# All sums on VectorE, attention steps spread over fixed units, and one output tile of block 0 split between two stages

## Chip, cores, metric

One core of a Trainium2 chip. The metric is device time in microseconds (us); several runs are taken, and all times compared here are of runs in the fast state (within 1.5% of the fastest run of the same kernel). The kernel before takes 316.09 us (median of 4 runs, 315.37 to 317.78).

## Reference

```python
kv  = einsum('bhsd,bhse->bhde', k, v)           # 8 batches, 8 heads, 576 positions, head size 64
o   = einsum('bhsd,bhde->bhse', q, kv)
x   = o / sqrt(mean(o*o, -1) + 1e-6) * g_norm   # as [4608 tokens, 512]
h   = x @ w_in                                  # [4608, 2048]
out = (max(h,0) + alpha*min(h,0)) @ w_out       # [4608, 512]
```

## The kernel before, where it matters

Tokens are handled in nine blocks of 512. In block w, sixteen *units* each make one hidden group of 128 rows (four matmuls, line 335; ScalarE and VectorE evict it into `gt`), seven output matmuls of block w-1 (line 486), and a share of the attention of block w+1. For a pair of heads the attention steps are `t` (transposes of q, line 236), `kv` (product of k and v, line 254), `ot` (q times kv, line 277) and `ssq` (sums of squares, line 293), after which VectorE writes `xt`, the input of the next block's hidden groups. To evict is to read a finished PSUM bank, so that it can be filled again. The output product is done with seven half-size products in place of eight, for which sums of activations (`s1` to `s4`) and of w_out (`wsum`) are needed. (In block 1, and in the stage before it, block 0's output is still made in the plain way, by line 360.) Two engines make the sums; GpSimd also issues nearly all loads and, from batch 2 on, regroups each loaded batch.

```python
# stage_p has bufs=2: a staging tile is free again when batch b-2 has been read from it
def load_main(b, nm, h0, h1): nc.gpsimd.dma_start(out=st, in_=...)             # q, k, v of a batch
def regroup(b, nm, h0, h1, eng): eng.tensor_copy(out=bufs[b % 3][nm]..., in_=stages[b, nm]...)
# v is not regrouped: step_kv reads vst, the staging tile, directly
...
def s_sum(w, n, k):
    if n == 1:   nc.vector.tensor_add(out=t, in0=a21, in1=a22)
    elif n == 2: nc.vector.tensor_sub(out=t, in0=sums[w,1,k], in1=a11)
    elif n == 3: nc.gpsimd.tensor_sub(out=t, in0=a11, in1=a21)
    else:        (nc.gpsimd if w == 1 else nc.vector).tensor_sub(out=t, in0=a12, in1=sums[w,2,k])
...
# PSUM bank Z takes product 5, is read ("c22") in unit 12, then takes product 3 (from unit 13 on)
Y_READS = {2: ("p1",), 5: ("u2",), 7: ("c11",), 9: ("u3",), 12: ("c22",), 14: ("c21",)}
...
for w in range(1, NW):
    if w + 2 < B: load_batch(w + 2)              # GpSimd's queue: k, v, q
    for u in range(NF):
        m1_group(w, G_ORDER[u])
        unit_sums(w, u)
        if w + 2 < B and u in (10, 12): regroup(w + 2, "k" if u == 10 else "q", 0, H, nc.gpsimd)
        ...                                      # seven prod_mm, then Y_READS
        while steps and n - len(steps) < want: steps.pop(0)()     # attention steps, as they fit
```

## Time and profile before

| | busy us of 314.3 | in the changed kernel, of 318.3 |
|---|---|---|
| TensorE (PE) | 287.0 | 290.4 |
| VectorE (DVE) | 219.3 | 231.7 |
| ScalarE (ACT) | 161.1 | 160.2 |
| GpSimd (POOL) | 127.2 | 62.9 |

How to read it: TensorE bounds the kernel, so what counts is what makes it wait, stage by stage. Below I measure a block from the start of its first line-335 matmul to the next block's, in TensorE's timeline. The lines of the profile that show the waits are in the prediction.

### The profile page before, as it was taken

What the parts mean: (1) busy time and instruction counts of PE and PEld (TensorE: products, weight loads), DVE (VectorE), ACT (ScalarE), POOL (GpSimd) and SP (SyncE); (2) the same over time, 40 slices, a digit from 0 to 9 for tenths busy, and PEclk for the clock granted to TensorE, in tenths of its full rate; (3) what the DMA queues carried; (4) which work ended last, traced back from release to release, by engine and by line L of the source; (5) the groups of instructions that cost most, each with busy time, mean ns of one, the idle gap of its engine ahead of it and who ended that gap; (6) DMA issues with size and microseconds to landing.
All of it is one profiled execution on the core that took longest, in us unless ns stands there. A gap on an engine that the chain in (4) does not pass through costs nothing.

```text
span 314.3 us, 5166 instructions
## 1 busy us (share of the span) xinstructions
PE 287.0 (91%) x1972; PEld 180.7 (57%) x1972; DVE 219.3 (70%) x373; ACT 161.1 (51%) x268; POOL 127.2 (40%) x118
## 2 busy tenths in 40 slices
PE   5778899696899999999999999999999999999992
PEld 1433354343466657665766576656665666666682
DVE  4358833758769886888688768876777778866831
ACT  2256556466455556555655555555654565444210
POOL 8424312999999551365136413311111112211100
PEclk9999999979799999999999999999999999999998
DMA  7999999790049199029902990111102110200233
GB/s 109 181 206 194 200 199 214 110 155 2 28 43 185 39 149 177 1 41 161 161 17 27 157 162 9 26 67 34 37 1 52 50 35 9 75 19 33 64 89 85
DMA packets 52552, 28.32 MB, mean 90 GB/s; under 512 B 15136, under 2 KB 52016, under 8 KB 52528
## 3 DMA queue, kind: packets, MB, share of 16 engines
q0 software_dynamic: 40320, 18.16, 45.8%
q1 hardware_dynamic: 11424, 9.19, 10.3%
q10 hardware_dynamic: 784, 0.66, 0.8%
q8 instruction: 15, 0.25, 0.3%
q14 instruction: 9, 0.07, 0.1%
HBM read 36.71 MB, written 9.44 MB: 147 GB/s over the span
## 4 chain that ended last, share of the span: by engine, by line
PE 76%; DVE 12%; ACT 5%; issue 2%; DMA 2%; SPq 1%; DVEq 0%
PE h_ps L335 34%; PE yY L486 11%; PE yZ L486 9%; PE yX L486 7%; DVE gt L346 4%; PE qt_ps L236 3%; DVE s L433 3%; ACT m_sb L342 3%; PE ot_ps L277 3%; PE ssq_ps L293 2%; PE kv_ps L254 2%; DMA alpha_row<-in_moe_alpha_dram 2%; DVE s L435 1%; ACT sq_sb L283 1%; DVE y_sb L513 1%
## 5 line engine op out<-in xcount | busy, mean ns | idle before, releaser
L335 PE MATMUL h_ps<-xt,w_in_sb 128*128 128x512 f16 x576 | 148.9, 384 | 2.2 <-DVE gt L346 1.4
L346 DVE SCALAR_TENSOR_TENSOR gt<-m_sb,beta_sb,h_ps 128x512 f16<-128x512 f32 x144 | 107.0, 744 | 56.7 <-ACT m_sb L342 55.3
L342 ACT ACTIVATE m_sb<-h_ps 128x512 f32<-128x512 f32 x144 | 85.9, 597 | 81.3 <-PE h_ps L335 73.5
L437 POOL TENSOR_TENSOR s<-gt 128x512 f16<-128x512 f16 x32 | 39.1, 1223 | 134.5 <-DVE gt L346 134.2
L335 PEld LDWEIGHTS <-w_in_sb 128*128 128x128 f16 x576 | 54.8, 99 | 55.3 <-issue 12.1
L486 PEld LDWEIGHTS <-s 128*128 128x128 f16 x512 | 50.1, 98 | 21.1 <-issue 1.9
L486 PEld LDWEIGHTS <-gt 128*128 128x128 f16 x384 | 37.6, 98 | 15.1 <-issue 0.4
L303 DVE SCALAR_TENSOR_TENSOR xt<-ot_ps,g2col,rstd 128x512 f16<-128x512 f32 x36 | 26.9, 746 | 12.2 <-ACT rstd L295 12.1
L486 PE MATMUL yX<-w_out_sb,gt 128*128 128x256 f16 x256 | 35.1, 273 | 0.1
L295 ACT ACTIVATE rstd<-ssq_ps,eps_t 128x512 f32<-128x512 f32 x36 | 24.7, 687 | 16.5 <-PE ssq_ps L293 16.3
L283 ACT ACTIVATE sq_sb<-ot_ps 128x512 f16<-128x512 f32 x36 | 21.4, 598 | 16.4 <-PE ot_ps L277 16.4
L248 ACT COPY qt_sb<-qt_ps 128x576 f16<-128x576 f16 x28 | 17.9, 638 | 15.3 <-PE qt_ps L236 15.3
L440 DVE TENSOR_TENSOR s<-gt,s 128x512 f16<-128x512 f16 x28 | 21.2, 758 | 0.0
L236 PE MATMUL qt_ps<-ident,qsb 128*128 128x128 f16 x160 | 14.5, 226 | 6.0 <-DVE kv_sb L262 5.2
L293 PE MATMUL ssq_ps<-sq_sb,mask 128*128 128x512 f16 x36 | 13.7, 382 | 5.8 <-ACT sq_sb L283 4.5
L433 DVE TENSOR_TENSOR s<-gt 128x512 f16<-128x512 f16 x32 | 18.8, 588 | 0.0
L486 PE MATMUL yY<-w_out_sb,s 128*128 128x256 f16 x128 | 18.7, 272 | 0.1
L486 PE MATMUL yZ<-w_out_sb,s 128*128 128x256 f16 x128 | 17.5, 272 | 0.7 <-DVE y_sb L513 0.3
L486 PE MATMUL yY<-wsum,s 128*128 128x256 f16 x128 | 17.6, 273 | 0.0
L486 PE MATMUL yZ<-wsum,s 128*128 128x256 f16 x128 | 17.6, 273 | 0.0
L486 PE MATMUL yY<-wsum,gt 128*128 128x256 f16 x128 | 17.6, 273 | 0.0
L236 PEld LDWEIGHTS <-qsb 128*128 128x128 f16 x160 | 11.8, 101 | 9.8 <-issue 5.9
(66 smaller groups left out, 263.9 us busy)
## 6 DMA issues: line engine op xcount, KB each, us to landing
out_dram<-y_sb SPq DMA_DIRECT2D x72, 64.0 KB, 2.2
kst<-in_k_dram POOLq DMA_DIRECT2D x7, 512.0 KB, 6.4
qst<-in_q_dram POOLq DMA_DIRECT2D x7, 512.0 KB, 11.8
vst<-in_v_dram POOLq DMA_DIRECT2D x7, 512.0 KB, 9.2
out_dram<-y_sb SPq DMA_DIRECT2D x23, 128.0 KB, 2.1
w_in_sb<-in_moe_w_in_dram POOLq DMA_DIRECT2D x4, 512.0 KB, 14.7
w_out_sb<-in_moe_w_out_dram POOLq DMA_DIRECT2D x4, 512.0 KB, 15.9
out_dram<-y_sb SPq DMA_DIRECT2D x4, 256.0 KB, 3.0
```

The lines of the kernel that those rows point to most:

```text
L236: nc.tensor.matmul(out=qt_ps[:, t * P : (t + 1) * P], lhsT=qs(t), rhs=ident16[:], is_transpose=True, start=(t == 0), stop=(t == NT - 1),)
L283: nc.scalar.activation(out=sq[:], in_=ot_ps[:], func=AF.Square)
L293: nc.tensor.matmul(out=ssq_ps[:], lhsT=mask16[:], rhs=sq[:], start=True, stop=True)
L295: nc.scalar.activation(out=rstd[:], in_=ssq_ps[:], func=AF.Abs_reciprocal_sqrt, bias=eps_t[:], scale=inv_d,)
L303: nc.vector.scalar_tensor_tensor(out=xts[w, j][:], in0=ot_ps[:], scalar=g2col[:], in1=rstd[:], op0=ALU.mult, op1=ALU.mult,)
L335: nc.tensor.matmul(out=h_ps[:], lhsT=w_in_blk(c, g), rhs=xts[w, c][:], start=(c == 0), stop=(c == NC - 1),)
L342: nc.scalar.activation(out=m_sb[:], in_=h_ps[:], func=AF.Relu, scale=-1.0)
L346: nc.vector.scalar_tensor_tensor(out=gts[w, i][:, r, :], in0=m_sb[:], scalar=beta_sb[:, g : g + 1], in1=h_ps[:], op0=ALU.mult, op1=ALU.add,)
L433: nc.vector.tensor_add(out=t[:], in0=a21, in1=a22)
L437: nc.gpsimd.tensor_sub(out=t[:], in0=a11, in1=a21)
L440: eng.tensor_sub(out=t[:], in0=a12, in1=sums[w, 2, k][:])
L486: nc.tensor.matmul(out=bank, lhsT=lhs, rhs=rhs, start=fresh, stop=(c == NK - 1), skip_group_check=True,)
```

## The change

Intent: sums cost less on VectorE and no longer lock it out of SBUF from GpSimd; attention steps that depend on each other lie units apart; and block 1, short of TensorE work, gets half of an output tile from the stage before it.

```diff
-            nc.gpsimd.tensor_sub(          # four kinds of w_out sums
+            nc.vector.tensor_sub(
 ...
-            nc.gpsimd.tensor_sub(out=t[:], in0=a11, in1=a21)
+            nc.vector.tensor_sub(out=t[:], in0=a11, in1=a21)
 ...
+    SPLIT = 8
+        ps_h.tile([P, W], FP32, name="yb", tag="h0"), ps_h.tile([P, W], FP32, name="yc", tag="h2"),
+    T_AT = {9: (1, 0), 11: (1, 1), 13: (2, 0), 15: (4, 0)}       # w_out sums in stage two
     for g in range(NF):
-        for a in range(AHEAD):
+        for a in range(AHEAD if g < SPLIT else AHEAD - 1):
 ...
-    regroup_batch(2)                                             # was on GpSimd
+    h_tags[0] = ("h0", "h1")
+    for j in range(NPAIR):
+        for what, at in (("t", 0), ("kv", 1), ("ot", 3), ("ssq", 5)):
+            ATT_AT.setdefault(3 * j + at, []).append((what, j))
 ...
+            if w == 1 and u in (0, 1):
+                regroup(2, "k" if u == 0 else "q", 0, H, nc.vector)
 ...
+                if u < NF - SPLIT:                               # block 1: rest of the third tile
+                    y_mm(ys[2], 0, 2, SPLIT + u)
-            while steps and n - len(steps) < want: steps.pop(0)()
+            attention(w + 1, u - shift)                          # shift = 1 in block 1
```

The regroups of batches 3 to 7 stay on GpSimd, at the same places in the program (units 10 and 12). Within a group of four units, the sums s3 and s4 move by up to two units.

More of the change, by code (lines that the diff above doesn't have):

```diff
@@ L410, in w_sum @@
         elif n == 2:
-            nc.gpsimd.tensor_sub(
+            nc.vector.tensor_sub(
                 out=wsum[2][:, sl, :], in0=w_hi(i, HC, D_MODEL), in1=wsum[1][:, sl, :]
@@ L414, in w_sum @@
         elif n == 4:
-            nc.gpsimd.tensor_sub(
+            nc.vector.tensor_sub(
                 out=wsum[4][:, sl, :], in0=w_hi(i, 0, HC), in1=wsum[2][:, sl, :]
@@ L418, in w_sum @@
         else:
-            nc.gpsimd.tensor_sub(
+            nc.vector.tensor_sub(
                 out=w_lo(i, HC, D_MODEL), in0=w_hi(i, HC, D_MODEL), in1=w_lo(i, HC, D_MODEL),
@@ L436, in s_sum @@
         elif n == 3:
-            nc.gpsimd.tensor_sub(out=t[:], in0=a11, in1=a21)
+            nc.vector.tensor_sub(out=t[:], in0=a11, in1=a21)
         else:
-            eng = nc.gpsimd if w == 1 else nc.vector
-            eng.tensor_sub(out=t[:], in0=a12, in1=sums[w, 2, k][:])
+            nc.vector.tensor_sub(out=t[:], in0=a12, in1=sums[w, 2, k][:])
     ybank = {}
@@ L577 @@
     AHEAD = 3
+    SPLIT = 8
     ys = [
         ps_y.tile([P, W], FP32, name="ya", tag="y"),
-        h_bank("yb"),
-        h_bank("yc"),
+        ps_h.tile([P, W], FP32, name="yb", tag="h0"),
+        ps_h.tile([P, W], FP32, name="yc", tag="h2"),
     ]
@@ L584, with attention @@
     n = len(steps)
+    T_AT = {9: (1, 0), 11: (1, 1), 13: (2, 0), 15: (4, 0)}
+    total = 2 * NF + SPLIT
+    done = 0
     for g in range(NF):
-        for a in range(AHEAD):
+        for a in range(AHEAD if g < SPLIT else AHEAD - 1):
             y_mm(ys[a], 0, a, g)
-            if a != 1 and steps and n - len(steps) < n * (AHEAD * g + a + 1) // (AHEAD * (NF - 3)):
+            done += 1
+            if steps and n - len(steps) < n * done // (total - 4):
                 steps.pop(0)()
-    for a in range(AHEAD):
+        if g in T_AT:
+            w_sum(*T_AT[g])
+    while steps:
+        steps.pop(0)()
+    for a in range(AHEAD - 1):
         y_out(ys[a], 0, a)
-    regroup_batch(2)
+    h_tags[0] = ("h0", "h1")
+    ssq_pool[0] = (ps_s, "s")
     def unit_sums(w, u):
         k, r = divmod(u, 4)
-        k -= 1
-        if k >= 0 and r < 3:
-            s_sum(w, (1, 2, 4)[r], k)
-            if r == 0:
-                s_sum(w, 3, k)
-    for w in range(1, NW):
-        steps = window_steps(w + 1) if w + 1 < NW else []
-        n = len(steps)
-        first_g = 4 if w == 1 else 0
-        if w == 2:
-            h_tags[0] = ("h0", "h1")
-            ssq_pool[0] = (ps_s, "s")
-            for i in range(2):
-                w_sum(3, i)
-        if 0 < w and w + 2 < B:
-            load_batch(w + 2)
-        if w == 1:
-            for i in range(2):
-                for m in (1, 2, 4):
-                    w_sum(m, i)
-        y = None
+        if k > 0:
+            s_sum(w, r + 1, k - 1)
+    ATT_AT = {}
+    for j in range(NPAIR):
+        for what, at in (("t", 0), ("kv", 1), ("ot", 3), ("ssq", 5)):
+            ATT_AT.setdefault(3 * j + at, []).append((what, j))
+    ATT = {"t": step_t, "kv": step_kv, "ot": step_ot, "ssq": step_ssq}
+    def attention(w, u):
+        if w < NW:
+            for what, j in ATT_AT.get(u, ()):
+                if w < B or what in ("ot", "ssq"):
+                    ATT[what](w, j)
+    for w in range(1, NW):
+        shift = 1 if w == 1 else 0
+        if w + 2 < B:
+            load_batch(w + 2)
         for u in range(NF):
@@ L620 @@
             unit_sums(w, u)
-            if w > 1 and u < 3:
+            if w > 1 and u < 4:
                 unit_sums(w - 1, NF + u)
+            if w == 2 and u in (1, 2):
+                w_sum(3, u - 1)
+            if w == 1 and u in (1, 3):
+                w_sum(2 if u == 1 else 4, 1)
             if w + 2 < B and u in (10, 12):
                 regroup(w + 2, "k" if u == 10 else "q", 0, H, nc.gpsimd)
+            if w == 1 and u in (0, 1):
+                regroup(2, "k" if u == 0 else "q", 0, H, nc.vector)
             if w > 2 and u == 0:
@@ L628 @@
                 if u == 0:
-                    y = ps_y.tile([P, W], FP32, name="y_ps", tag="y")
-                y_mm(y, 0, AHEAD, u)
+                    yd = ps_y.tile([P, W], FP32, name="yd", tag="y")
+                if u < NF - SPLIT:
+                    y_mm(ys[2], 0, 2, SPLIT + u)
+                    if u == NF - SPLIT - 1:
+                        y_out(ys[2], 0, 2)
+                y_mm(yd, 0, AHEAD, u)
                 if u == NF - 1:
-                    y_out(y, 0, AHEAD)
+                    y_out(yd, 0, AHEAD)
             else:
@@ L637 @@
                     y_read(w - 1, what)
-            want = n * (u - first_g + 1) // (NF - 2 - first_g)
-            while steps and n - len(steps) < want:
-                steps.pop(0)()
+            attention(w + 1, u - shift)
     w = NW - 1
@@ L644 @@
     for u in range(NF):
-        if u < 3:
+        if u < 4:
             unit_sums(w, NF + u)
```

## The prediction

> **What bounds the kernel now.** I read first the page, then the windows view with one window for each stage, then TensorE's waits, then the timeline inside the stages that lose time. The page has TensorE (PE) busy for 287.0 of 314.3 us and VectorE (DVE) for 219.3, so the bound is TensorE, and a change can only win what TensorE spends waiting. I cut the span at the first hidden-layer matmul (line 335) of each token block. Columns: stretch, its length, then busy us of PE, PE weight loads, DVE, ACT and POOL, granted clock, DMA share, GB/s.
>
> ```profile
> 36.50:52.40 15.90, 15.02 (x102) 7.73 (x100) 6.17 (x11) 8.31 (x14) 3.48 (x4) 1.00 1.43 198
> 52.40:83.95 31.55, 25.30 (x134) 11.95 (x132) 22.20 (x29) 17.36 (x31) 28.47 (x20) 0.89 0.59 87
> 83.95:116.50 32.55, 30.79 (x228) 20.17 (x227) 27.25 (x39) 18.86 (x32) 26.52 (x24) 1.00 0.79 99
> 147.80:178.96 31.16, 30.39 (x230) 20.56 (x228) 24.19 (x42) 18.01 (x31) 13.41 (x12) 1.00 0.62 91
> 210.12:241.28 31.16, 30.39 (x230) 20.40 (x228) 22.27 (x42) 18.01 (x31) 4.71 (x4) 1.00 0.12 36
> ```
>
> The rows are stage two (output of block 0), block 1, block 2, block 4 and block 6. Block 1 stands out: PE is busy 25.30 of 31.55 us, part of that at a granted clock of 0.89 on average, and GpSimd (POOL) is busy nearly throughout. TensorE's waits over the whole run (total us, times, longest) name two things worth having:
>
> ```profile
> PE qt_ps L236 <- DVE kv_sb L262: 5.2, 3, 2.7
> PE ssq_ps L293 <- ACT sq_sb L283: 4.5, 7, 0.7
> ```
>
> The second comes once in each of the attention windows 1 to 7. The first is in blocks 1 and 2, and its longest instance reads so in the timeline:
>
> ```profile
> 59.07 1.95 DVE L433 TENSOR_TENSOR s<-gt 128x512 f16<-128x512 f16 x1
> 60.94 0.73 DVE L346 SCALAR_TENSOR_TENSOR gt<-m_sb,beta_sb,h_ps 128x512 f16<-128x512 f32 x1
> 61.94 0.28 DVE L262 TENSOR_TENSOR kv_sb<-kv_ps,mask 128x128 f16<-128x128 f32 x1
> 62.27 0.44 PE L236 MATMUL qt_ps<-ident,qsb 128*128 128x128 f16 x5 [2.67 <-DVE kv_sb L262]
> ```
>
> An activation sum that usually takes 0.42 us took 1.95; the small kv eviction queued behind it, kv and the next transpose share one PSUM bank, and PE stood 2.67 us. The tile view of the sums shows how unusual that is (min/median/max ns), and what the same sum costs on POOL:
>
> ```profile
> L433 DVE TENSOR_TENSOR s<-gt x32: 408/418/1946, 59.1 to 297.0; 128x512 f16<-128x512 f16 x32
> L435 DVE TENSOR_TENSOR s<-s,gt x32: 410/418/1684, 61.6 to 297.9; 128x512 f16<-128x512 f16 x32
> L437 POOL TENSOR_TENSOR s<-gt x32: 1148/1204/1330, 75.0 to 293.4; 128x512 f16<-128x512 f16 x32
> ```
>
> **What the Trainium skill says.** "SBUF — State Buffer", section "SBUF: two separate sides": VectorE and GpSimd share a port pair as an exclusive lock, and a VectorE op with two SBUF inputs contends with a GpSimd op that reads SBUF for its whole length. The trace agrees: the long sums lie mostly beside POOL's sums, weight sums and regroups (a 2.41 us DVE sum at 99.31 beside a 1.88 us regroup at 99.56); the one at 59.07 lies beside DMA issues, which the rule doesn't clearly cover. "GPSIMD Engine Reference", section "Engine selection", puts two-input elementwise work at about twice VectorE's time on GpSimd; here it is 1204 against 418 ns, near three times. "TensorE: Matmul & The Clock Gate", section "Part 1: The HAM clock gate", says that an idle window halves TensorE's clock: after the 2.67 us wait, line 335's matmuls run some 0.43 us apart from 62.5 to 66 instead of 0.22, and again from 80 to 84.
>
> **The change part by part.**
>
> *Sums to VectorE.* Off POOL go 32 sums of line 437 (39.1 us), 4 of line 440 (5.0), 8 weight sums (17.4) and two regroups of batch 2 (3.8). Onto DVE come 36 x 0.418 = 15.0 us, 8 weight sums, and two regroups (0.69 to 0.95 each by the two 128x2048 copies DVE does already). A weight sum has twice the columns; line 516 (256 f32 columns, 0.42 us) and line 513 (512, 0.68) give 0.16 us fixed, so I estimate 0.16 + 2 x 0.26 = 0.69 us, 5.5 in all. Added: 22 us. Removed: lines 433, 435 and 440 now cost 18.8 + 17.2 + 21.2 = 57.2 us for 92 sums, against 38.5 at 0.418, so up to 18.7 us of lock waiting. DVE's busy total stays near 220 us; that it loses its long blockages is what counts. POOL keeps only DMA issues and ten regroups of 1.89 us, each of which can still hold up one sum by a microsecond or so.
>
> *Steady blocks 3 to 6.* One unit is 4 matmuls of line 335 (0.86 us start to start) and 7 of line 486 (0.76): 16 units are 26.0. Attention adds 4 x (0.28 + 0.28 + 0.22 + 0.22) = 4.0. So 30.0 of TensorE work in 31.16 us. The rest is the block's last pair of steps, placed back to back:
>
> ```profile
> 174.43 0.38 PE L277 MATMUL ot_ps<-qt_sb,kv_sb 128*128 128x320 f16 x2
> 175.49 0.38 PE L293 MATMUL ssq_ps<-sq_sb,mask 128*128 128x512 f16 x1 [0.69 <-ACT sq_sb L283]
> ```
>
> From the end of ot's slot (174.65) to ssq's start (175.49) 0.84 us go by, and about 0.25 at the first yZ of unit 13, behind DVE's read of the bank (173.47 + 0.68). With ot at unit 3j+3 and ssq at 3j+5 two units (over 3.2 us) lie between them, and the 0.84 goes; transposes, kv and ssq, which share a bank, also get a unit each. The 0.25 stays. Each of four blocks gains 0.8: **3.2 us**. DVE then has 16 x 0.66 to 0.745 (gt), 16 x 0.42, 4 x 0.28, 4 x 0.75, 5 x 0.68 = 26 us of 30.3: fuller, but TensorE still leads. Block 7 has no such wait now: 0.1.
>
> *Block 2.* 32.55 us with the same 30.0 of work. Blocked sums, the 0.78 us transpose wait and ssq's 0.7 go. Two weight sums (1.4 us) and the new sums bring DVE to some 28 to 29 of 30.6, so I keep 0.6 of loss: **1.9 us**.
>
> *Stage two.* 8 output matmuls x 0.216 move out: 1.7 us. Denser steps give back some: kv of pair 0 comes two matmuls after its transpose, not three, +0.2; the first hidden group waits about 0.25 for its last xt, as only four output matmuls follow ssq. It ends near 50.95, not 52.40: **1.45 us**.
>
> *Block 1.* TensorE work: 13.8 (line 335) + 24 x 0.216 + 4.0 = 23.0 us. DVE: 11.9 (gt) + 12 x 0.42 + 2 x 0.69 + 1.6 (regroups) + 1.1 + 3.0 = 24.0, plus 2 for regroups on POOL: so DVE and TensorE are nearly level. Two new waits come. First, the regroup of q sits at unit 1, about 53.5, but POOL's regroup shows those data landing only at 55.17; the first transpose follows at once in TensorE's order. DVE does a weight sum and the regroup after that, so the transpose starts about 56 to 57: a wait of 2.4 to 3.1 us, perhaps with 1.7 us of half clock after it. Second, block 1 is shifted by one, so its last ssq is in unit 15, and block 2's first group needs that xt: rstd 0.69 + xt 0.75 + a y copy of 0.58 ahead on ACT, less what TensorE has to do, is about 1.6 us. So 23.0 + 2.7 + 1.6 + 0.9 (half the chance of the slow clock) + 1.3 for DVE queueing = 29.5, against 31.55: **2.0 us**.
>
> Sum: 3.2 + 0.1 + 1.9 + 1.45 + 2.0 = 8.7 us, that is 316.07 - 8.7 = 307.4. Batch 2 might land earlier in the new order of POOL's queue, which would take away the first new wait, so I move to **307.0 us**.
>
> **The rivals.** (a) *VectorE becomes the bound.* Against: 26 of 30.3 us in a steady block, with 0.8 us between the eviction of a group and the reuse of its bank two units later. For: there are only two hidden banks, and blocks 1 and 2 are level. If blocks 2 to 5 lost a microsecond each, 311. (b) *The waits of block 1 take the place of those removed*: the late q data cost a full 3 us, the clock halves, DVE queues behind: nothing gained in block 1, 309 to 310. (c) *Everything fits*: q data come in time, block 1 runs at its work of some 25 us, steady blocks at 30.2: 302 to 303. (d) *Removing POOL's sums changes nothing since DVE is off the path*: true for blocks 3 to 6, where DVE has 7 us to spare, so there the spacing of the steps must give the gain; this rival leaves about 311.
>
> **Range and chances.** The steady gain is read directly from a wait, so 3 us are nearly sure; block 1 may give from 0 to 6.5. From these 303 to 310.5. Two per cent faster is below 309.7: 0.81; within two per cent 0.18; slower 0.01.
>
> **What would show it.** The wait of ssq for sq gone from blocks 2 to 6 and these at 30.2 to 30.5 us; lines 433, 435, 437 and 440 on DVE with medians near 0.42 and few over 1 us; weight sums near 0.7 us; stage two ending near 51; in block 1 a wait of the first transpose for the regroup of q near 55 to 57, and one of block 2's first group for xt. Steady blocks above 31 us with waits on gt would prove (a); block 1 over 31 us, (b); block 1 under 27 us with no wait on q, (c).

## The result

The changed kernel takes 319.89 us (319.25 to 320.2, 4 runs), ratio 1.011 with a 95% interval of 1.0067 to 1.0153: some 1% slower, inside the two per cent that count as the same, and not faster. (A ratio is the mean time of one kernel's runs over that of the other's of the same rounds, so not quite the ratio of the medians.)

TensorE's waits in the changed kernel (us in total, times, longest; lines left out are marked):

```profile
PE yZ L485 <- DVE y_sb L512: 6.9, 4, 2.5
...
PE qt_ps L236 <- DVE qsb L148: 2.8, 2, 2.2
...
PE h_ps L335 <- DVE xt L303: 2.1, 3, 1.3
...
PE h_ps L335 <- ACT y_sb L387: 0.9, 1, 0.9
...
PE ssq_ps L293 <- ACT sq_sb L283: 0.3, 1, 0.3
```

The two waits that the change aimed at have gone: ssq's for sq is down from 4.5 to 0.3 us, the transposes' for kv is off the list. At the top stands one that had been 0.3: product 3 waits for VectorE's read of its bank Z (c22, line 512). The windows of the changed kernel, stage two and blocks 1 to 5 (columns as in the prediction):

```profile
37.09:52.58 15.49, 13.54 (x93) 6.95 (x92) 7.64 (x14) 9.33 (x15) 5.43 (x8) 1.00 1.43 197
52.58:81.40 28.82, 25.73 (x140) 12.41 (x140) 21.85 (x39) 16.04 (x28) 11.14 (x10) 0.94 1.03 136
81.40:116.86 35.46, 32.06 (x229) 21.19 (x228) 28.57 (x47) 19.13 (x33) 11.12 (x11) 0.95 0.66 90
116.86:150.99 34.13, 32.05 (x230) 21.24 (x228) 27.11 (x47) 17.88 (x31) 8.88 (x9) 0.95 0.57 84
150.99:185.43 34.44, 31.92 (x231) 21.17 (x229) 26.81 (x46) 17.88 (x31) 7.20 (x7) 0.95 0.57 83
185.43:215.68 30.25, 30.24 (x231) 20.44 (x229) 23.76 (x46) 17.88 (x31) 0.00 (x0) 1.00 0.13 36
```

Block 5, without GpSimd work, takes 30.25 us, as predicted for a steady block. Blocks 2 to 4, with it, take 34 to 35.5, and their granted clock is below full. What happens there is the same each time; the changed kernel's timeline in block 3 (GpSimd's and VectorE's lines, and TensorE's at the end):

```profile
138.69 0.88 POOL L131 DMA_DIRECT2D vst<-in_v_dram  x1 [20.42 <-PE kv_ps L254]
...
140.23 0.91 POOL L131 DMA_DIRECT2D qst<-in_q_dram  x1
140.64 2.68 DVE L439 TENSOR_TENSOR s<-gt,s 128x512 f16<-128x512 f16 x1
141.10 1.93 POOL L148 COPY ksb<-kst 128x2048 f16<-128x2048 f16 x1
...
143.25 0.74 DVE L303 SCALAR_TENSOR_TENSOR xt<-ot_ps,g2col,rstd 128x512 f16<-128x512 f32 x1
143.91 0.73 DVE L346 SCALAR_TENSOR_TENSOR gt<-m_sb,beta_sb,h_ps 128x512 f16<-128x512 f32 x1
144.57 0.41 DVE L433 TENSOR_TENSOR s<-gt 128x512 f16<-128x512 f16 x1
144.90 0.68 DVE L512 TENSOR_TENSOR y_sb<-yZ,u 128x512 f32<-128x512 f32 x1
145.63 0.38 PE L485 MATMUL yZ<-w_out_sb,s 128*128 128x256 f16 x2 [2.08 <-DVE y_sb L512]
```

Read it downwards. GpSimd has stood 20.42 us: its next load of v needs a staging tile that the fourth kv step, in unit 10, has just read for the last time. Released, it issues v and q and goes straight into the regroup of k, whose data landed long ago. (This is batch 6, whose regroup stands in block 4 of the program and ran there before: GpSimd now runs a block ahead, which is also why block 5 has no regroup left.) Beside it a sum of unit 11 that takes 0.42 us takes 2.68. Four shorter VectorE operations queue behind it, the last of which is the read of bank Z, and TensorE waits 2.08 us for that.

In the kernel before, GpSimd's own sums, which wait for `gt`, decide when its queue gets to the regroups. GpSimd's timeline in block 4 of the kernel before:

```profile
159.79 1.27 POOL L437 TENSOR_TENSOR s<-gt 128x512 f16<-128x512 f16 x1 [6.29 <-DVE gt L346]
161.01 1.89 POOL L148 COPY ksb<-kst 128x2048 f16<-128x2048 f16 x1
167.57 1.27 POOL L437 TENSOR_TENSOR s<-gt 128x512 f16<-128x512 f16 x1 [4.68 <-DVE gt L346]
168.79 1.89 POOL L148 COPY qsb<-qst 128x2048 f16<-128x2048 f16 x1
```

The second regroup is over at 170.7. It too lengthens a sum, but the read of bank Z comes only at 173.47, and TensorE waited 0.25; VectorE's timeline there:

```profile
169.32 1.64 DVE L440 TENSOR_TENSOR s<-gt,s 128x512 f16<-128x512 f16 x1
...
173.47 0.68 DVE L513 TENSOR_TENSOR y_sb<-yZ,u 128x512 f32<-128x512 f32 x1
```

### The profile page after: what moved, and what is told of

The parts are those of the page before. It is cut to its first block, busy times and chain, and to the rows that moved or that the text cites.

```text
span 318.3 us, 5127 instructions
## 1 busy us (share of the span) xinstructions
PE 290.4 (91%) x1972; PEld 182.7 (57%) x1972; DVE 231.7 (73%) x419; ACT 160.2 (50%) x268; POOL 62.9 (20%) x72
## 4 chain that ended last, share of the span: by engine, by line
PE 78%; DVE 11%; ACT 5%; DMA 2%; issue 2%; SPq 1%; DVEq 0%
PE h_ps L335 34%; PE yY L485 12%; PE yZ L485 9%; PE yX L485 8%; DVE gt L346 4%; PE qt_ps L236 3%; PE kv_ps L254 3%; ACT m_sb L342 3%; PE ssq_ps L293 3%; PE ot_ps L277 2%; DMA alpha_row<-in_moe_alpha_dram 2%; DVE xt L303 2%; ACT rstd L295 1%; PE yc L360 1%; DVE s L439 1%
## 5 line engine op out<-in xcount | busy, mean ns | idle before, releaser
L485 PEld LDWEIGHTS <-s 128*128 128x128 f16 x512 | 51.1, 100 | 29.2 <-issue 9.8
L283 ACT ACTIVATE sq_sb<-ot_ps 128x512 f16<-128x512 f32 x36 | 21.3, 597 | 15.7 <-PE ot_ps L277 15.5
L485 PE MATMUL yZ<-w_out_sb,s 128*128 128x256 f16 x128 | 19.9, 297 | 7.0 <-DVE y_sb L512 6.9
L131 POOL DMA_DIRECT2D vst<-in_v_dram x9 | 7.7, 858 | 64.2 <-PE kv_ps L254 60.8
L485 PE MATMUL yY<-w_out_sb,s 128*128 128x256 f16 x128 | 18.7, 272 | 0.1
L236 PE MATMUL qt_ps<-ident,qsb 128*128 128x128 f16 x160 | 15.2, 234 | 2.9 <-DVE qsb L148 2.8
L437 DVE TENSOR_TENSOR s<-gt 128x512 f16<-128x512 f16 x32 | 17.4, 545 | 0.0
L293 PE MATMUL ssq_ps<-sq_sb,mask 128*128 128x512 f16 x36 | 14.6, 406 | 2.1 <-ACT rstd L295 1.1
L254 PEld LDWEIGHTS <-ksb 128*128 128x128 f16 x160 | 12.1, 102 | 5.7 <-issue 2.6
```

The lines of the kernel that those rows point to most:

```text
L236: nc.tensor.matmul(out=qt_ps[:, t * P : (t + 1) * P], lhsT=qs(t), rhs=ident16[:], is_transpose=True, start=(t == 0), stop=(t == NT - 1),)
L254: nc.tensor.matmul(out=kv_ps[:], lhsT=ks(t), rhs=vs(t), start=(t == 0), stop=(t == NT - 1),)
L283: nc.scalar.activation(out=sq[:], in_=ot_ps[:], func=AF.Square)
L293: nc.tensor.matmul(out=ssq_ps[:], lhsT=mask16[:], rhs=sq[:], start=True, stop=True)
L485: nc.tensor.matmul(out=bank, lhsT=lhs, rhs=rhs, start=fresh, stop=(c == NK - 1), skip_group_check=True,)
```

## Experiments

Theory T: the loss is the regroup's new place: GpSimd's queue, no longer paced by sums, is released at unit 10 to 11 and locks out a sum that stands ahead of the read of bank Z. Rival R: VectorE has too much to do. Nine kernels ran; all gave correct results. Block lengths in us from the profiled run of each:

| kernel | stage two | 1 | 2 | 3 | 4 | 5 | 6 | median us | ratio to before [95%] |
|---|---|---|---|---|---|---|---|---|---|
| before | 15.87 | 31.55 | 32.75 | 31.10 | 31.16 | 31.16 | 31.17 | 316.09 | |
| changed | 15.49 | 28.82 | 35.46 | 34.13 | 34.44 | 30.25 | 30.24 | 319.89 | 1.011 [1.0067, 1.0153] |
| e1 regroups on VectorE | 15.49 | 27.49 | 32.94 | 31.32 | 30.94 | 30.95 | 30.25 | 309.87 | 0.981 [0.979, 0.984] |
| e2 v loaded last | 15.49 | 33.76 | 35.75 | 34.26 | 34.25 | 30.25 | 30.25 | 322.96 | 1.021 [1.018, 1.025] |
| e3 regroups before v | 15.49 | 27.41 | 35.28 | 30.25 | 30.24 | 30.25 | 30.25 | 310.90 | 0.984 [0.981, 0.988] |
| e4 spacing only | 15.95 | 31.08 | 32.88 | 30.75 | 30.81 | 30.82 | 30.31 | 313.23 | 0.992 [0.990, 0.994] |
| e5 sums only | 15.87 | 28.94 | 35.24 | 36.59 | 35.40 | 31.43 | 31.43 | 326.46 | 1.036 [1.030, 1.042] |
| e6 block 1 reworked | 14.39 | 25.95 | 30.76 | 30.38 | 30.24 | 30.25 | 30.25 | 303.31 | 0.961 [0.957, 0.965] |
| e7 bank turn | 14.39 | 27.98 | 35.32 | 32.32 | 36.01 | 30.25 | 30.25 | 318.45 | 1.006 [1.000, 1.012] |
| e8 sums late | 15.70 | 31.62 | 31.31 | 30.32 | 30.21 | 30.21 | 30.20 | 308.75 | 0.976 [0.970, 0.982] |
| e9 sums, safe queue | 15.87 | 30.72 | 32.34 | 32.64 | 32.64 | 31.43 | 31.43 | 316.54 | 1.003 [1.001, 1.004] |

The medians are of all runs; e7 and e9 have one slow run each, and the medians of their fast runs are 317.25 and 316.51.

### e1: the regroups on VectorE

```diff
-    regroup(w + 2, "k" if u == 10 else "q", 0, H, nc.gpsimd)
+    regroup(w + 2, "k" if u == 10 else "q", 0, H, nc.vector)
```

> The changed kernel, with the regroups of batches 3 to 7 on VectorE instead of GpSimd (same places in the program). Theory T: in blocks 2 to 4 the GpSimd regroup of k starts at unit 11 of the block, because its queue is held by the v load until the fourth kv step of unit 10; it locks out the fourth sum of unit 11 for 2 to 3 us, VectorE's read of bank Z (c22) comes late and TensorE waits 2.1 to 2.5 us at the first yZ of unit 13, then runs at half clock. T expects no such wait over 0.5 us, blocks 2 (after its first wait for xt), 3 and 4 near 30.3 us as blocks 5 and 6, no sum over 1 us in them, and 308 to 311 us in all. Rival R (VectorE simply has too much to do in blocks 2 to 4 once it has all sums): this adds some 1.6 us of VectorE work to each block, so blocks 2 to 4 stay at 34 us or get longer, and the time is 320 us or more.

309.87 us. VectorE got *more* work and the kernel became 10 us faster: R falls. The waits at yZ are 0.7 us at most (expected 0.5), since the regroup of q stands in unit 12 right ahead of the read; the granted clock is 1.00 throughout the profiled run. Blocks 3 to 5 take 30.9 to 31.3 us, not the 30.3 expected: those waits are still there.

### e2: v loaded last

```diff
-            load_batch(w + 2)
+            load_batch(w + 2, ("k", "q", "v"))
```

> The changed kernel, loads of batches 3 to 7 in the order k, q, v instead of k, v, q; the regroups stay on GpSimd. Now k and q have landed long before the v load lets GpSimd's queue go on at unit 10 to 11, so both regroups run one behind the other there. T expects two blocked sums in units 11 and 12 ahead of the read of bank Z: the wait at yZ in blocks 2 to 4 grows from 2.1-2.5 to 3-4.5 us, and the time to 322 to 326 us. R expects no difference (319 to 321 us).

322.96 us, in the range, but not for the reason written. In blocks 2 to 4 the wait at yZ was 2.3 us, about as in the changed kernel (2.1 to 2.5), since one sum, not two, was blocked. From the timeline of this run, around unit 11 of block 3:

```profile
143.71 1.91 POOL L148 COPY ksb<-kst 128x2048 f16<-128x2048 f16 x1
...
144.79 2.94 DVE L439 TENSOR_TENSOR s<-gt,s 128x512 f16<-128x512 f16 x1
...
145.54 1.91 POOL L148 COPY qsb<-qst 128x2048 f16<-128x2048 f16 x1
...
150.03 0.38 PE L485 MATMUL yZ<-w_out_sb,s 128*128 128x256 f16 x2 [2.34 <-DVE y_sb L512]
```

The sum begins in the first regroup, is still held when that ends, and gets through only after the second: these two GpSimd copies in a row did not let VectorE in between. The regroup of k now starts over 1 us ahead of the sum, so the total is nearly the same. The loss is in block 1 instead, 5 us longer: there such a pair held a sum for 4.37 us, the kv eviction behind it came late, and TensorE waited 4.31 us for it.

### e3: regroups queued before the load of v

```diff
-            load_batch(w + 2)
+            load_batch(w + 2, ("k", "q"))
+            regroup(w + 2, "k", 0, H, nc.gpsimd)
+            regroup(w + 2, "q", 0, H, nc.gpsimd)
+            load_batch(w + 2, ("v",))
```

(and the regroups at units 10 and 12 taken out)

> The changed kernel, with GpSimd's queue for batches 3 to 7 in the order load k, load q, regroup k, regroup q, load v. The regroups stay on GpSimd and cost the same lock, but they come when k and q have landed, some 8 to 12 us after unit 10 to 11, so about unit 15 and unit 0 to 2 of the next block, behind the read of bank Z. T expects the wait at yZ gone or under 0.5 us, single blocked sums of 1 to 2 us that TensorE doesn't notice or notices by less than 1 us, and 308 to 312 us. A rival T2 (any GpSimd work that reads SBUF costs a block 3 to 4 us now that VectorE is fuller, wherever it lies) expects 318 us or more; R expects 319 to 321.

310.90 us: as T expected. GpSimd does the same copies, now around the change of blocks; single sums still take up to 1.86 us, and blocks 3 and 4 take 30.25 us all the same. So not GpSimd's work but its moment costs. Block 2 missed: 35.28 us. It begins with a wait of 2.22 us for the last xt, for here a regroup (78.74 to 80.83) held a sum at the change of blocks; a second held sum (1.41 us) cost 0.90 us at yY; and part of the block ran at half clock.

### e4: spacing only, on the kernel before

```diff
-        steps = window_steps(w + 1) if w + 1 < NW else []
+        steps = window_steps(w + 1) if w == 1 else []
 ...
+            if w > 1: attention(w + 1, u)      # ATT_AT as in the change
```

> The kernel before, with one part of the change alone: in blocks 2 to 7 the attention steps at fixed units (transpose 3j, kv 3j+1, ot 3j+3, ssq 3j+5); sums stay on GpSimd, block 1 and stage two as before. The prediction's reading of the steady blocks expects the wait of ssq for sq (0.7 us) gone from them, blocks 3 to 6 at 30.2 to 30.5 us instead of 31.16, and 311.5 to 313.5 us in all. If instead the kv step at unit 10 now lets GpSimd's queue start regroups at a bad place here too, blocks 3 and 4 show a wait at yZ and the time is 315 us or more.

313.23 us, in the range. Block 6, without regroups, is at 30.31 us; blocks 3 to 5 are at 30.8, some 0.3 above what was expected: there ssq waits 0.3 us for the kv eviction, behind a sum that a regroup had lengthened to 1.4 us. With GpSimd still paced by its sums there is no wait at yZ over 0.3. (In block 2 a sum that took 2.35 us beside GpSimd's own sums cost 1.64 us at yY.)

### e5: sums only, on the kernel before

```diff
-            nc.gpsimd.tensor_sub(      # all w_out sums, s3, and s4 of block 1
+            nc.vector.tensor_sub(
```

> The kernel before, with the other part of the change alone: all activation and weight sums on VectorE; attention steps, stage two, block 1 and the regroups of batch 2 on GpSimd as before. T expects block 1 to gain 2 to 4 us (no weight sums on GpSimd beside its sums), and in blocks 2 to 4 that GpSimd, which no sum paces any more, starts the regroup of k some 2.5 us after the fourth kv step of unit 11, that is in unit 12 to 13, beside the sum of unit 12 or after it; the read of bank Z is then mostly through. So blocks 3 and 4 at 31 to 32.5 us with ssq's wait of 0.7 still there, and 311 to 315 us. If all sums on VectorE are harmful in themselves, blocks 5 and 6, which have no regroup, get longer than 31.2 us.

326.46 us: a miss, in T's favour in kind and against my guess of the place. This half of the change alone makes the kernel 3.6% slower. The attention steps are where they were, so GpSimd is released in unit 11, and the regroup meets the sum of unit 12, the last operation but one ahead of the read of bank Z (timeline of this run, VectorE, then TensorE):

```profile
178.28 3.12 DVE L433 TENSOR_TENSOR s<-gt 128x512 f16<-128x512 f16 x1
182.38 0.38 PE L486 MATMUL yZ<-w_out_sb,s 128*128 128x256 f16 x2 [3.05 <-DVE y_sb L513]
```

Blocks 5 and 6, without regroups, are 0.27 us longer than before: the added sums by themselves cost that little.

### e8: the sums of units 11 and 12 made in unit 13

```diff
-            unit_sums(w, u)
+            for x in () if w > 1 and u in (11, 12) else (11, 12, 13) if w > 1 and u == 13 else (u,):
+                unit_sums(w, x)
```

> The changed kernel, but in blocks 2 to 8 the activation sums of units 11 and 12 are made in unit 13; every regroup stays on GpSimd in its old place. If theory T has the chain right (GpSimd's regroup locks out the sum of unit 11, this holds up VectorE's read of bank Z in unit 12, this holds up yZ in unit 13), the lock now hits nothing that stands ahead of the read: wait at yZ under 0.5 us in blocks 2 to 4, blocks 3 and 4 at 30.3 to 31 us, 308 to 311 us in all. If the lock costs TensorE through something else (evictions gt, the bank that transposes share), blocks 3 and 4 stay at 33 us or more and the time at 317 or more.

308.75 us (305.49 to 309.77); blocks 3 and 4 at 30.3 and 30.2. The regroup starts where it did, and nothing that TensorE needs stands behind a two-input VectorE operation. From this run, GpSimd's line and then VectorE's:

```profile
108.04 1.91 POOL L148 COPY ksb<-kst 128x2048 f16<-128x2048 f16 x1
```

```profile
108.75 0.75 DVE L346 SCALAR_TENSOR_TENSOR gt<-m_sb,beta_sb,h_ps 128x512 f16<-128x512 f32 x1
109.42 0.68 DVE L512 TENSOR_TENSOR y_sb<-yZ,u 128x512 f32<-128x512 f32 x1
```

The eviction (0.75) and the read (0.68), each with an input in PSUM, run at their usual length inside the regroup. That agrees with the Trainium skill, "SBUF — State Buffer", section "SBUF: two separate sides", which names a VectorE operation with two SBUF inputs as the one that contends with GpSimd's reads: beside GpSimd's copies and sums only VectorE's sums grew in these traces. This closes the chain: lock, sum, read of bank Z, yZ. (Block 1, whose sums this run leaves in place, shows the lock again: a sum at 76.55 takes 2.68 us, the regroup of k running from 77.02, and the evictions `gt` behind it come late: TensorE waits 2.06 us.)

### e7: block 1's first bank

```diff
     h_tags[0] = ("h0", "h1")
+    h_turn[0] = 0
```

> The changed kernel, with one line more: block 1 takes its first hidden group in bank h1 instead of h0, which yb has just filled. In the changed kernel this first group waits 0.94 us for ScalarE's copy of yb. Expected: that wait gone, the first regroups and the transpose's wait some 0.6 us earlier, 319.0 to 319.5 us; stage two ends near 51.6 us after a start at 37.1, thus 14.6 us long. If the wait only moves into the wait of the first transpose for the regroup of q, stage two is as short but nothing is gained in all.

Stage two is 14.39 us, not 15.49: the wait of 0.94 us for ScalarE's copy of yb is gone. In the whole it can't be told: three runs of 316.1 to 319.7 us and a slow one, against the changed kernel's 319.9 of other rounds. The run settles something else, the share of the clock. Blocks 3 and 4 of this run:

```profile
113.02:145.34 32.32, 30.24 (x231) 20.62 (x228) 25.52 (x44) 17.85 (x31) 6.62 (x7) 1.00 0.60 89
145.34:181.35 36.01, 32.07 (x230) 21.13 (x228) 29.46 (x48) 17.88 (x31) 9.08 (x9) 0.95 0.54 79
```

Block 3 here has the same wait of 2.08 us at yZ as in the changed kernel, keeps its full clock, and takes 32.32 us against 34.13 at 0.95. So of the 3.9 us that block 3 of the changed kernel loses against block 5, 2.1 are the wait and 1.8 the half clock that follows it. It doesn't simply add up over a run: block 4 here starts with a wait of 1.42 us for xt, behind a sum that the regroup of q held for 2.03 us, that the changed kernel's trace does not have, and one timed run of the changed kernel with a mean clock of 0.995 was only 0.8 us shorter than the profiled one with 0.966. For that run there is no trace.

### e9: sums only, with e3's queue

```diff
  (e5, with the four lines of e3 in place of load_batch(w + 2), and without its regroups at units 10 and 12)
```

> The sums-only kernel (the kernel before with all sums on VectorE, 326.5 us), with GpSimd's queue for batches 3 to 7 in the order load k, load q, regroup k, regroup q, load v. Attention steps still in their old places. If sums on VectorE are harmless and the place of the regroups was all that made that kernel slow, the waits at yZ fall under 0.5 us, blocks 3 to 6 are all near 31.2 to 31.4 us (ssq's wait of 0.7 us is still there), and the time is 311 to 314 us. If all sums on VectorE cost by themselves, it stays above 318.

316.54 us, 10 us better than e5, but short of the 311 to 314 expected. The waits at yZ are down to 0.35 us in blocks 2 to 6 (0.6 at the longest, later); blocks 5 and 6 are at 31.43, as in e5. But blocks 3 and 4 are at 32.64: with the attention steps in their old places, close together, the regroup of k now holds a sum (2.11 us) ahead of a kv eviction, and the next transpose waits 1.05 us. Putting the sums on VectorE gains nothing by itself, even with a harmless queue at yZ; it needs the spacing too.

### e6: e3 with block 1 reworked

```diff
-    T_AT = {9: (1, 0), 11: (1, 1), 13: (2, 0), 15: (4, 0)}
+    T_AT = {5: (1, 0), 7: (1, 1), 9: (2, 0), 10: (4, 0), 12: (2, 1), 14: (4, 1)}
+    h_turn[0] = 0
+    # attention in block 1: t 3,5,8,11; kv 4,6,9,12; ot 5,8,11,13; ssq 7,10,13,14
-            if w == 1 and u in (1, 3): w_sum(2 if u == 1 else 4, 1)
-            if w == 1 and u in (0, 1):           # regroups of batch 2
+            if w == 1 and u in (0, 2):
```

> An attempt to beat both kernels: regroups ahead of the v load as in the run of that name, the first bank of block 1 turned, all six weight sums of stages two and one spread over stage two, the regroup of q for batch 2 in unit 2, and block 1's attention steps in units 3 to 14, so that neither its first transpose waits for the regroup nor block 2 for the last xt. T expects block 1 at 25 to 26.5 us (27.4 in that run), block 2 at 30.5 to 32 (35.3), blocks 3 to 6 at 30.25, and 303 to 306 us. If VectorE is the real bound of block 1, it stays above 27 us and the time above 308.

303.31 us (302.56 to 304.28), as expected, and 3.9% faster than the kernel before. Its windows for blocks 1, 2 and 3:

```profile
50.45:76.40 25.95, 24.18 (x142) 11.53 (x141) 22.17 (x37) 17.29 (x32) 8.41 (x8) 1.00 1.17 154
76.40:107.16 30.76, 30.55 (x230) 20.51 (x229) 27.70 (x48) 18.89 (x32) 16.89 (x16) 1.00 0.98 123
107.16:137.54 30.38, 30.37 (x230) 20.61 (x228) 25.90 (x46) 17.86 (x31) 8.62 (x8) 1.00 0.64 95
```

TensorE is busy in all but 0.2 us of block 2 and nearly all of block 3, though VectorE has 25.9 to 27.7 us in them: it is full, but not the bound.

## Why the prediction was wrong

**Right.** The work of a steady block is 30.0 us and the back-to-back pair cost 0.84: blocks 5 and 6 came out at 30.25, in the 30.2 to 30.5 named. Sums on VectorE have a median of 0.418 us, weight sums take 0.68 (0.69 estimated). Block 1's new waits were there, both a little shorter: 2.25 us for the regroup of q (2.4 to 3.1 predicted), 1.31 for the last xt (1.6). The first came from VectorE's queue alone; it went from a weight sum straight into the regroup and did not wait for data.

**Wrong: the step on GpSimd.** The prediction said: "POOL keeps only DMA issues and ten regroups of 1.89 us, each of which can still hold up one sum by a microsecond or so." Two things failed. *Size*: the sum at the fourth kv step takes 2.68 to 3.12 us in place of 0.42, so it is held up by 2.3 to 2.7; the 2.41 us sum that the prediction quotes from the kernel before was a warning of that. Over the run the sums on VectorE take 65.9 us against 53.5 at 0.418 each, so 12.4 us of waiting at the lock are there, where up to 18.7 were to be removed, and VectorE's busy total is 231.7 us, not near 220. *Place*, which matters more: I took the regroups to stay where the program has them and a delay to vanish in VectorE's slack of some 4 us a block. But GpSimd's operations run in order, each when those ahead of it let go. With the sums taken off, the last thing that holds GpSimd is the load of v, which waits for a kv step; and the spacing fixes that step at unit 10, two units ahead of the read of bank Z. What counts is not VectorE's slack over the block but that of the one operation that TensorE needs next. e3 and e8 show both ends of it: move the regroup, or move the sum, and 9 to 11 us come back.

By stages, predicted against measured lengths (block 2's wait for xt moved into block 2): stage two 14.4 and 15.5, block 1 27.9 and 28.8, block 2 32.5 and 35.5, blocks 3 and 4 30.4 each and 34.1 and 34.4, blocks 5 and 6 30.4 and 30.2. The differences sum to 12.6 us; from the 307.4 worked out to the 319.9 measured it is 12.5. Of it 10.9 are in blocks 2 to 4. (For block 2 I start from its 32.75 us; the prediction's window, 32.55, ends 0.2 us short of the next block.) There the three waits at yZ make 6.7 us, and half clock after them, which the prediction allowed for in block 1 alone, some 1.8 each by e7's measure.

**Wrong: stage two.** Sized at 1.45 us of gain, it gave 0.4: I missed that block 1's first hidden group takes yb's bank and waits for its copy. e7 shows the 1.1 us.

**Rivals.** (a), VectorE as the bound, was refuted by e1. (d), that the gain comes from the spacing alone, fits e4 (0.8%) and e9 best as to the parts, but it gave 311 for the whole; no rival had a part that loses. Neither (b) nor (c) came: block 1 took 28.8 us, between their 31 and 27. That the sums alone lose 3.6% only e5 showed.

**Open.** It stays open why the lock takes in the issue of a load just ahead of the regroup (below); a load's issue alone did not do it at 138.74, where a sum beside the issue of v took 0.42 us. Whether the half clock costs as much in every run is not settled.

## What to carry to other kernels

When you take work off an engine with an in-order queue, ask what paced what is left on it: find what it will wait for now, at which moment that lets go, and what the next operation in its queue collides with. Average slack on the other engine says nothing here; look for the short operation in front of a buffer that the bound engine needs next. And measure each half of a change alone: here one half gave 0.8%, the other lost 3.6%, and with the queue's order repaired the whole gave 1.6%, and 3.9% after the first block was reworked.

## What the Trainium skill lacked or had wrong

- "SBUF — State Buffer", section "SBUF: two separate sides": it says that whichever starts first gets the shared ports for its whole instruction. In the changed kernel the sum starts by its record at 140.64, before the regroup at 141.10, and yet ends after it at 143.32; GpSimd's records are rough, so this is a doubt and no proof.
- The same section doesn't say what happens between GpSimd instructions in a row, and it differs: in e2 a sum was held across two copies, for 2.94 us; in the kernel before a sum got in between two weight sums (it ended at 70.75, the first of them at 70.46, the second at 72.73).
- "GPSIMD Engine Reference", section "Engine selection": two-input work is put at about twice VectorE's time; here a sum takes 1204 ns on GpSimd and 418 on VectorE, 2.9 times.
- "TensorE: Matmul & The Clock Gate", section "Part 1: The HAM clock gate": it gives an idle window of about 3.4 us for the half clock. Here waits of 2.08 us, shorter than that, were followed by it in the changed kernel's block 3 (1.8 us lost) and not in e7's block 3.
- On no page I read: that an in-order GpSimd queue which issues loads and also computes has its compute moved by the loads' waits (14 to 21 us of standing in blocks 2 to 4 before the load of v, and with it the regroup of k).
